# Attention forward and backward on one core: operands in quarter tiles, the normalisation's place, and where the constant matmuls stand

## The chip, the cores and the metric

The kernel runs on one core of a Trainium2 chip. The metric is device time in microseconds (us) of one execution. Five engines work side by side, each through its own instructions in order: TensorE (PE; PEld is its weight load), VectorE (DVE), ScalarE (ACT), GpSimd (POOL) and SyncE (SP), which in this kernel issues every DMA.

## The reference

The reference is the forward and backward pass of a gated mix of two branches over 2048 tokens of width 576. The changed part is branch A, an attention with 32 heads of width 18, and its gradients:

```python
qkv = (x @ wqkv).reshape(B, S, 3, H, Dh)          # S = 2048, H = 32, Dh = 18
scores = einsum("bhqd,bhkd->bhqk", q, k) * Dh ** -0.5
p = softmax(scores)
o = einsum("bhqk,bhkd->bhqd", p, v)
a = o.transpose(...).reshape(B, S, D) @ wo
...
return g * a + (1 - g) * b                        # g: a gate per token; b: an SSM convolution
```

The outputs are the result and the gradients of all inputs of both branches. Branch B, the projections and the weight gradients are other stages of the kernel and are not changed.

## The kernel before

The attention stage lies between 251 and about 2466 us of the profiled execution. Heads are padded to 32 columns, so a **group** g is four heads side by side on 128 partitions; there are 8 groups. Queries are cut into four blocks b of 512. A **unit** u = 4g + b is one group with one query block: 32 units, forward and backward. For a unit all 2048 keys are swept in 16 tiles i of 128.

The stage is one loop over a counter `G`. I call one turn of it a **half-step**; 32 half-steps (`NST`) are a unit. In one half-step the forward of unit u runs beside the backward of an earlier one, which is 39 half-steps behind (`OFF`, and `G2 = G - OFF`). PE, ACT, DVE and POOL run in the order in which the code records their instructions (`manual_schedule`). SP is not in that list: a scheduler orders the DMAs by its own estimate of when each is ready, and SP then works through that order one by one.

A half-step records, in this order:

- what was put off to it with `at(("pre", G), ...)`: gradient stores (`store_grad`: ACT copies `gb`, SP transposes it into `gT`, POOL copies it to `dtk`, SP stores that) and, once a unit, `f1` and `f2` (below);
- six score matmuls on PE, three kinds twice: P1 (key tile against the unit's queries, for the forward), P3 (query tile against 512 keys, for the backward) and P2 (value tile against `dOaT`). P1 and P3 share four PSUM buffers with the tag S, P2 has two with the tag dP;
- a **burst**: constant matmuls of `J_bf` with the identity (`fill`, `NFILL` of them; their result is written over or not used), and accumulations. The number `ph = G2 % 4` names four kinds of half-step, and four of them I call a cycle. In ph 0, the **value** half-step: accO (forward output, 4 matmuls), then accV (`dv_burst`, 8). In ph 1, the **query** half-step: accO, then accQ (`dq_burst`, 8). In ph 2, the **key** half-step: accK (`dk_half` twice, 16). In ph 3, the **free** half-step: only constants, into accF. accV, accQ, accK and accF share one PSUM bank (accB), and each burst starts with its `NFILL[ph]` constants;
- on ACT four exponentials of 128x512 (L611 for P1 into `PT`, L615 for P3 into `eb`), on DVE two products (L620, `ds` from P2's result and `PT`), whose transposes `dsT` SP issues (L626); then the evictions of the burst on DVE (`dvacc` L473, `dqa` L490, `dkacc` L514).

Once a unit, when accO is complete, `post_forward` gives three functions. `f0` copies accO to `oT` on ACT. `f1`, two half-steps later and ahead of the score matmuls, transposes `oT` back with four matmuls into `ps_o`, a PSUM buffer of the tag S, and then on DVE takes the reciprocal `rl` (L399), the normalised output `Ob` (L404) and the scaled output gradient `dOa` (L405). `f2`, one half-step later, multiplies the two into `prod` (L410), reduces it to `dl` (L412), writes that into `dOa` (L413) and issues two DMAs, the store `O_d` and the transpose `dOaT`, which the backward's P2 rows read from half-step 39 on.

`load_group(g)` brings a group's operands: `QaT`, `KaT` and `VaT` as they are and `Vtok`, `Ktok` and `Qtok` through a transposing DMA, each 128 x 2048 in one piece. All have two buffers but `Ktok` (read by accQ) and `Qtok` (read by accK), which have one. The load for the next group is recorded in a group's third unit.

Of the kernel before, what the change touches and what calls it, by code (L numbers as in the profile page):

```python
# [9 lines left out]
A = mybir.AluOpType  # L10
ACT = mybir.ActivationFunctionType
BF = mybir.dt.bfloat16
# [8 lines left out]
def build(tc, aps, dbg_aps=None, stages=("s1", "attn", "post", "s4", "final")):  # L21
# [39 lines left out]
    with ExitStack() as gctx:  # L61
# [281 lines left out]
        if "attn" in stages:  # L343
# [3 lines left out]
            DA = HP  # L347
            NFILL = (1, 1, 1, 4)
            with ExitStack() as ctx:
# [14 lines left out]

                def load_group(g):
                    T = {}
                    for nm, src, nb in (("QaT", QaT_d[g], 2), ("KaT", KaT_d[g], 2), ("VaT", VaT_d[g], 2)):
                        T[nm] = ga.tile([P, S], BF, tag=nm, bufs=nb, name=nm + "_g")
                        nc.sync.dma_start(T[nm], src)
                    for nm, src, nb in (("Vtok", VaT_d[g], 2), ("Ktok", KaT_d[g], 1), ("Qtok", QaT_d[g], 1)):  # L370
                        T[nm] = ga.tile([P, NT, 4, HP], BF, tag=nm, bufs=nb, name=nm + "_g")
                        nc.sync.dma_start_transpose(out=T[nm].rearrange("p t h w -> p t (h w)"), in_=src)
                    grp_t[g] = T

# [11 lines left out]
                def post_forward(g, b, acc):  # L386
                    U = UN[(g, b)]
                    st = {}

                    def f0():  # L390
                        st["oT"] = work.tile([P, KB], F32, tag="oT", bufs=1, name="oT")
                        nc.scalar.copy(st["oT"], acc)

                    def f1():
                        po = apsp.tile([P, TPQ, 4, HP], F32, tag="S", bufs=4, name="ps_o")
                        for qi in range(TPQ):
                            nc.tensor.transpose(po[:, qi, :, :].rearrange("p a b -> p (a b)"), st["oT"][:, qi * P:(qi + 1) * P], ident_f)
                        rl = work.tile([P, TPQ, 4], F32, tag="rl", bufs=1, name="rl")
                        nc.vector.reciprocal(rl, po[:, :, :, DH])  # L399
                        rlb = rl.unsqueeze(3).to_broadcast([P, TPQ, 4, DH])  # L400
                        Ob = work.tile([P, TPQ, 4, DH], BF, tag="Ob", bufs=1, name="Ob")
                        da = U["dOa"]
                        st["Ob"] = Ob
                        nc.vector.tensor_tensor(Ob, po[:, :, :, 0:DH], rlb, op=A.mult)  # L404
                        nc.vector.tensor_tensor(da[:, :, :, 0:DH], U["dO"], rlb, op=A.mult)  # L405

                    def f2():
                        da, Ob = U["dOa"], st["Ob"]
                        prod = work.tile([P, TPQ, 4, DH], F32, tag="prod", bufs=1, name="prod")
                        nc.vector.tensor_tensor(prod, da[:, :, :, 0:DH], Ob, op=A.mult)  # L410
                        dl = work.tile([P, TPQ, 4], F32, tag="dl", bufs=1, name="dl")
                        nc.vector.tensor_reduce(dl, prod, axis=AX.X, op=A.add)  # L412
                        nc.vector.tensor_scalar(da[:, :, :, DH], dl, -1.0, None, op0=A.mult)  # L413
                        nc.sync.dma_start(O_d[:, b * TPQ:(b + 1) * TPQ, 4 * g * DH:4 * (g + 1) * DH], Ob.rearrange("p t a b -> p t (a b)"))
                        U["dOaT"] = work.tile([P, TPQ, P], BF, tag="dOaT", name="dOaT")
                        nc.sync.dma_start_transpose(out=U["dOaT"], in_=U["dOa"].rearrange("p t a b -> p (t a b)"))
                    return f0, f1, f2
# [58 lines left out]
                def dq_burst(g, b, p):  # L476
                    U = UN[(g, b)]
                    acc = ACC.pop()
                    for n_ in range(2):
                        i = 2 * p + n_  # L480
                        for j in range(4):
                            mm(acc[HP * j:HP * (j + 1), :], lhsT=grp_t[g]["Ktok"][:, i, j, :], rhs=U["ds"][i][:, j, :],
                               start=(n_ == 0), stop=(n_ == 1), tile_position=(0, HP * j))
# [9 lines left out]
                def dk_half(g, b, p, h, st):  # L493
# [4 lines left out]
                    for qb in (2 * h, 2 * h + 1):  # L498
                        for j in range(4):
                            mm(acc[HP * j:HP * (j + 1), 0:2 * P].rearrange("p (a b) -> p a b", b=P), lhsT=grp_t[g]["Qtok"][:, b * TPQ + qb, j, :],  # L500
                               rhs=U["dsT", p][:, :, j * TPQ + qb, :], start=(qb == 0), stop=(qb == 3), tile_position=(0, HP * j))
# [14 lines left out]

                load_group(0)
                NTOT = NU * NST
                for G in range(NTOT + OFF + 16):
# [3 lines left out]
                    if G < NTOT:  # L523
# [5 lines left out]
                        if s == 4 and b == NQ - 2 and g + 1 < NG:  # L529
                            load_group(g + 1)  # L530
                        r1 = (g, b, s // 2, 2 * (s % 2))
# [8 lines left out]
                    for x in range(2):  # L540
                        if r1:
                            g, b, i, j0 = r1
                            T = grp_t[g]
                            rows.append(("P1", g, b, i, j0 + x, row("P1", g, b, T["KaT"][:, i * P:(i + 1) * P], T["QaT"][:, b * KB:(b + 1) * KB], j0 + x)))
                        if r2:
# [5 lines left out]
                            kq, ii = s2 // 8, (s2 % 8) // 2  # L551
                            qt = b * TPQ + ii
                            rows.append(("P3", g, b, (kq, ii), jo, row("P3", g, b, T["QaT"][:, qt * P:(qt + 1) * P], T["KaT"][:, kq * KB:(kq + 1) * KB], jo)))
                            i2 = s2 // 2
                            j2 = 2 * par_ + (1 - x)
                            rows.append(("P2", g, b, i2, j2, row("P2", g, b, T["VaT"][:, i2 * P:(i2 + 1) * P], U["dOaT"].rearrange("p t q -> p (t q)"), j2)))
                    evs = []
                    if G % 4 in (3, 0) and G >= 3:
                        i_ = (G - 3) // 4 * 2 + (1 if G % 4 == 0 else 0)
                        u_, i_ = divmod(i_, NT)  # L560
                        if u_ < NU:
# [3 lines left out]
                            for j in range(4):  # L565
                                mm(accO[(g, b)][HP * j:HP * (j + 1), :], lhsT=grp_t[g]["Vtok"][:, i_, j, :], rhs=UN[(g, b)]["PT"][i_][:, j, :],
                                   start=(i_ == 0), stop=(i_ == NT - 1), tile_position=(0, HP * j))
                            if i_ == NT - 1:
                                f0, f1, f2 = post_forward(g, b, accO.pop((g, b)))
                                evs.append(f0)  # L570
                                at(("pre", G + 2), f1)
                                at(("pre", G + 3), f2)
                    if ph in (0, 1, 2):
                        ACC.append(accB(("accV", "accQ", "accK")[ph]))
                        fill(ACC[0], NFILL[ph])
                    elif 0 <= G2 < NTOT:
                        fill(accB("accF"), NFILL[3])
                    if G2 % 4 == 0 and G2 >= 4:
# [27 lines left out]
                    for (kind, g, b, i, j, ps) in rows:  # L606
# [5 lines left out]
                        elif kind == "P3":  # L612
                            e = work.tile([P, KB], BF, tag="eb", bufs=10, name="eb")
                            U["eb"][(i[0], i[1], j)] = e
# [735 lines left out]
```

## Time and the profile before

| | |
|---|---|
| time, median of 9 runs | 3860.94 us (3854.22 to 3865.70) |
| the profiled execution | 3863.19 us, its span 3861.5 us |
| busy share of the span | PE 76%, DVE 75%, ACT 73%, POOL 2% |
| attention exponentials on ACT | 4096, 644 and 650 ns each by their rows |
| `ds` products on DVE | 2048, 686 ns each |
| constant matmuls | 256 each in accV, accQ and accK, 1040 in accF |

The span is the time from the first to the last instruction; 1.7 us of the execution lie around it. ACT and DVE overlap one instruction with the next, so a row's mean duration is longer than the distance between two of them. The distance between the ends of instructions that follow each other tells the pace.

### The profile page before, as it was taken

What the parts mean: (1) busy time and instruction counts of PE and PEld (TensorE: products, weight loads), DVE (VectorE), ACT (ScalarE), POOL (GpSimd) and SP (SyncE); (2) the same over time, 40 slices, a digit from 0 to 9 for tenths busy, and PEclk for the clock granted to TensorE, in tenths of its full rate; (3) what the DMA queues carried; (4) which work ended last, traced back from release to release, by engine and by line L of the source; (5) the groups of instructions that cost most, each with busy time, mean ns of one, the idle gap of its engine ahead of it and who ended that gap; (6) DMA issues with size and microseconds to landing.
All of it is one profiled execution on the core that took longest, in us unless ns stands there. A gap on an engine that the chain in (4) does not pass through costs nothing. (4 is left out here: it accounts for less than half of the span.)

```text
span 3861.5 us, 67450 instructions
## 1 busy us (share of the span) xinstructions
PE 2950.7 (76%) x25828; PEld 1164.3 (30%) x25828; DVE 2915.1 (75%) x5131; ACT 2830.8 (73%) x5253; POOL 62.8 (2%) x146
## 2 busy tenths in 40 slices
PE   7979999999989989989989999499244455444421
PEld 2312322323323323323223232146133333333320
DVE  4617877878878878878878888444388888888867
ACT  4549999999999999999989998310366666666610
POOL 0000000000000000000000000100000000000000
PEclk9959999999999999999999999789555555555555
DMA  8537788888887797887887887965455565655456
GB/s 198 166 99 126 139 159 144 143 159 142 145 162 136 142 165 138 143 163 136 145 159 135 147 145 135 242 155 135 84 98 106 106 108 111 113 97 103 84 147 198
DMA packets 1860151, 537.00 MB, mean 139 GB/s; under 512 B 1774991, under 2 KB 1838553, under 8 KB 1859826
## 3 DMA queue, kind: packets, MB, share of 16 engines
q1 hardware_dynamic: 1859826, 532.69, 71.8%
q8 instruction: 202, 3.31, 0.3%
q14 instruction: 123, 1.01, 0.1%
HBM read 99.74 MB, written 60.96 MB: 42 GB/s over the span
## 5 line engine op out<-in xcount | busy, mean ns | idle before, releaser
L620 DVE TENSOR_TENSOR ds<-ps_P,PT 128x512 bf16<-128x512 f32 x2048 | 1343.9, 686 | 181.9 <-PE ps_P L30 176.2
L611 ACT ACTIVATE PT<-ps_P 128x512 bf16<-128x512 f32 x2048 | 1308.3, 644 | 75.8 <-PE ps_P L30 68.5
L615 ACT ACTIVATE eb<-ps_P 128x512 bf16<-128x512 f32 x2048 | 1326.4, 650 | 22.6 <-PE ps_P L30 22.5
L30 PE MATMUL ps_P<-KaT_g,QaT_g 32*128 32x512 bf16 x2048 | 749.4, 384 | 55.8 <-ACT PT L611 4.4
L30 PE MATMUL ps_P<-dOaT,VaT_g 32*128 32x512 bf16 x2048 | 781.3, 390 | 5.9 <-DMA dOaT<-dOa 5.0
L30 PE MATMUL ps_P<-QaT_g,KaT_g 32*128 32x512 bf16 x2048 | 663.9, 392 | 18.9 <-DMA KaT_g<-KaT_d 5.8
L30 PEld LDWEIGHTS <-VaT_g 32*128 32x128 bf16 x2048 | 180.3, 91 | 368.6 <-issue 354.8
L30 PEld LDWEIGHTS <-J_bf 128*128 128x128 bf16 x1872 | 162.5, 98 | 397.9 <-issue 301.0
L30 PE MATMUL accF<-ident_bf,J_bf 128*128 128x512 bf16 x1040 | 277.6, 390 | 0.0
L30 PEld LDWEIGHTS <-KaT_g 32*128 32x128 bf16 x2048 | 122.1, 93 | 401.9 <-issue 388.3
L473 DVE TENSOR_TENSOR dvacc<-dvacc,accV 128x512 f32<-128x512 f32 x224 | 153.7, 686 | 95.2 <-PE accV L30 94.4
L30 PE MATMUL uvp<-RX,E1e 128*128 128x64 bf16 x1152 | 134.1, 290 | 107.6 <-DVE E1e L919 107.6
L30 PE MATMUL accO<-PT,Vtok_g 128*32 128x512 bf16 x2048 | 212.3, 399 | 0.0
L30 PE MATMUL tps<-RX,T0w 128*128 128x32 bf16 x576 | 38.4, 233 | 213.8 <-DVE yd L1054 190.4
L900 ACT ACTIVATE kk<-ph,magc 128x512 f32<-128x512 f32 x144 | 91.0, 685 | 147.6 <-DVE E1e L918 112.8
L30 PE MATMUL ph<-thr,lrow 3*128 3x512 bf16 x288 | 126.3, 567 | 87.9 <-ACT ab L893 60.5
L30 PEld LDWEIGHTS <-QaT_g 32*128 32x128 bf16 x2048 | 158.5, 91 | 112.0 <-issue 95.8
L30 PE MATMUL accK<-dsT,Qtok_g 128*32 128x256 bf16 x4096 | 164.5, 282 | 27.8 <-DMA Qtok_g<-QaT_d 25.1
L490 DVE TENSOR_TENSOR dqa<-dqa,accQ 128x512 f32<-128x512 f32 x224 | 153.9, 687 | 32.5 <-PE accQ L30 21.1
L30 PE MATMUL accQ<-ds,Ktok_g 128*32 128x512 bf16 x2048 | 160.0, 389 | 13.4 <-DMA Ktok_g<-KaT_d 13.4
L30 PEld LDWEIGHTS <-E1e 128*128 128x128 bf16 x1152 | 125.2, 123 | 128.3 <-DVE E1e L919 127.8
L30 PE MATMUL accV<-eb,dOa 128*32 128x512 bf16 x2048 | 157.8, 385 | 0.0
(271 smaller groups left out, 3767.6 us busy)
## 6 DMA issues: line engine op xcount, KB each, us to landing
T0w<-Kp_d SPq DMA_DIRECT2D x36, 512.0 KB
dsT<-ds SPq DMA_TRANSPOSE x512
dqkv_d<-dtk SPq DMA_DIRECT2D x96, 72.0 KB
dqkv_tok<-dqkv_d SPq DMA_DIRECT2D x1, 6912.0 KB
Md_d<-mst SPq DMA_DIRECT2D x144, 36.0 KB
ga_d<-ga_st SPq DMA_DIRECT2D x16, 288.0 KB
dxm_d<-dxm SPq DMA_DIRECT2D x16, 288.0 KB
skw<-Md_d SPq DMA_DIRECT2D x72, 64.0 KB
```

The costliest lines, as they stand in the source:

```text
L30: return nc.tensor.matmul(out, lhsT=lhsT, rhs=rhs, start=start, stop=stop, **kw)
L473: nc.vector.tensor_tensor(a_, a_, acc, op=A.add)
L490: nc.vector.tensor_tensor(U["dqa"], U["dqa"], acc, op=A.add)
L611: nc.scalar.activation(U["PT"][i][:, j, :], ps, ACT.Exp)
L615: nc.scalar.activation(e, ps, ACT.Exp)
L620: nc.vector.tensor_tensor(U["ds"][i][:, j, :], ps, U["PT"][i][:, j, :], op=A.mult)
L900: nc.scalar.activation(B_["kk"][h][:, 4 * q:4 * q + 4, :], ph, ACT.Identity, bias=magc, scale=1.0)
```

## The change

The change has these parts.

- `load_group` is replaced. `KaT` stays in one piece of 2048 columns with two buffers (`load_full`). The other five operands come in quarter pieces of 512 columns (`load_piece`), each a tile of its own, with 3 buffers for `QaT`, 5 for `VaT`, `Vtok` and `Ktok`, and 2 for `Qtok`. Each piece is recorded 14 to 20 half-steps ahead of the half-step for which it is listed. All readers take the piece.
- `f1` no longer runs ahead of the score matmuls. Its transposes go into the accF bank, behind the constants of the free half-step. `rl` and `Ob` stay on DVE, recorded after that half-step's `ds` products; `dOa` and `prod` move from DVE to POOL.
- `f2` no longer makes `prod`. It is recorded among the evictions of the next half-step, ahead of dvacc.
- `NFILL` goes from (1, 1, 1, 4) to (0, 1, 1, 5).
- `eb` gets 12 buffers in place of 10.

```diff
--- before.py
+++ after.py
@@ -345,7 +345,7 @@
             NQ = S // KB
             TPQ = KB // P
             DA = HP
-            NFILL = (1, 1, 1, 4)
+            NFILL = (0, 1, 1, 5)
             with ExitStack() as ctx:
                 ctx.enter_context(tc.manual_schedule(engines={mybir.EngineType.PE, mybir.EngineType.Activation, mybir.EngineType.DVE, mybir.EngineType.Pool}))
                 ga = ctx.enter_context(tc.tile_pool(name="ga", bufs=2))
@@ -362,15 +362,22 @@
                     dOa2.append(dOa_u)
                 grp_t = {}
 
-                def load_group(g):
-                    T = {}
-                    for nm, src, nb in (("QaT", QaT_d[g], 2), ("KaT", KaT_d[g], 2), ("VaT", VaT_d[g], 2)):
-                        T[nm] = ga.tile([P, S], BF, tag=nm, bufs=nb, name=nm + "_g")
-                        nc.sync.dma_start(T[nm], src)
-                    for nm, src, nb in (("Vtok", VaT_d[g], 2), ("Ktok", KaT_d[g], 1), ("Qtok", QaT_d[g], 1)):
-                        T[nm] = ga.tile([P, NT, 4, HP], BF, tag=nm, bufs=nb, name=nm + "_g")
-                        nc.sync.dma_start_transpose(out=T[nm].rearrange("p t h w -> p t (h w)"), in_=src)
-                    grp_t[g] = T
+                PB = {"QaT": 3, "VaT": 5, "Vtok": 5, "Ktok": 5, "Qtok": 2}
+
+                def load_full(g):
+                    t_ = ga.tile([P, S], BF, tag="KaT", bufs=2, name="KaT_g")
+                    nc.sync.dma_start(t_, KaT_d[g])
+                    grp_t.setdefault(g, {})["KaT"] = t_
+
+                def load_piece(nm, g, m):
+                    src = {"QaT": QaT_d, "VaT": VaT_d, "Vtok": VaT_d, "Ktok": KaT_d, "Qtok": QaT_d}[nm][g][:, m * KB:(m + 1) * KB]
+                    if nm in ("QaT", "VaT"):
+                        t_ = ga.tile([P, KB], BF, tag=nm, bufs=PB[nm], name=nm + "_g")
+                        nc.sync.dma_start(t_, src)
+                    else:
+                        t_ = ga.tile([P, TPQ, 4, HP], BF, tag=nm, bufs=PB[nm], name=nm + "_g")
+                        nc.sync.dma_start_transpose(out=t_.rearrange("p t h w -> p t (h w)"), in_=src)
+                    grp_t.setdefault(g, {})[nm, m] = t_
 
                 UN = {}
                 DKV = {}
@@ -391,23 +398,25 @@
                         st["oT"] = work.tile([P, KB], F32, tag="oT", bufs=1, name="oT")
                         nc.scalar.copy(st["oT"], acc)
 
-                    def f1():
-                        po = apsp.tile([P, TPQ, 4, HP], F32, tag="S", bufs=4, name="ps_o")
+                    def f1(po):
                         for qi in range(TPQ):
-                            nc.tensor.transpose(po[:, qi, :, :].rearrange("p a b -> p (a b)"), st["oT"][:, qi * P:(qi + 1) * P], ident_f)
-                        rl = work.tile([P, TPQ, 4], F32, tag="rl", bufs=1, name="rl")
-                        nc.vector.reciprocal(rl, po[:, :, :, DH])
-                        rlb = rl.unsqueeze(3).to_broadcast([P, TPQ, 4, DH])
-                        Ob = work.tile([P, TPQ, 4, DH], BF, tag="Ob", bufs=1, name="Ob")
-                        da = U["dOa"]
-                        st["Ob"] = Ob
-                        nc.vector.tensor_tensor(Ob, po[:, :, :, 0:DH], rlb, op=A.mult)
-                        nc.vector.tensor_tensor(da[:, :, :, 0:DH], U["dO"], rlb, op=A.mult)
+                            nc.tensor.transpose(po[:, qi * P:(qi + 1) * P], st["oT"][:, qi * P:(qi + 1) * P], ident_f)
+                        po = po.rearrange("p (t a b) -> p t a b", a=4, b=HP)
+
+                        def ev():
+                            rl = work.tile([P, TPQ, 4], F32, tag="rl", bufs=1, name="rl")
+                            nc.vector.reciprocal(rl, po[:, :, :, DH])
+                            rlb = rl.unsqueeze(3).to_broadcast([P, TPQ, 4, DH])
+                            Ob = st["Ob"] = work.tile([P, TPQ, 4, DH], BF, tag="Ob", bufs=1, name="Ob")
+                            nc.vector.tensor_tensor(Ob, po[:, :, :, 0:DH], rlb, op=A.mult)
+                            da = U["dOa"]
+                            nc.gpsimd.tensor_tensor(da[:, :, :, 0:DH], U["dO"], rlb, op=A.mult)
+                            prod = st["prod"] = work.tile([P, TPQ, 4, DH], F32, tag="prod", bufs=1, name="prod")
+                            nc.gpsimd.tensor_tensor(prod, da[:, :, :, 0:DH], Ob, op=A.mult)
+                        return ev
 
                     def f2():
-                        da, Ob = U["dOa"], st["Ob"]
-                        prod = work.tile([P, TPQ, 4, DH], F32, tag="prod", bufs=1, name="prod")
-                        nc.vector.tensor_tensor(prod, da[:, :, :, 0:DH], Ob, op=A.mult)
+                        da, Ob, prod = U["dOa"], st["Ob"], st["prod"]
                         dl = work.tile([P, TPQ, 4], F32, tag="dl", bufs=1, name="dl")
                         nc.vector.tensor_reduce(dl, prod, axis=AX.X, op=A.add)
                         nc.vector.tensor_scalar(da[:, :, :, DH], dl, -1.0, None, op0=A.mult)
@@ -479,7 +488,7 @@
                     for n_ in range(2):
                         i = 2 * p + n_
                         for j in range(4):
-                            mm(acc[HP * j:HP * (j + 1), :], lhsT=grp_t[g]["Ktok"][:, i, j, :], rhs=U["ds"][i][:, j, :],
+                            mm(acc[HP * j:HP * (j + 1), :], lhsT=grp_t[g]["Ktok", i // TPQ][:, i % TPQ, j, :], rhs=U["ds"][i][:, j, :],
                                start=(n_ == 0), stop=(n_ == 1), tile_position=(0, HP * j))
 
                     def ev():
@@ -497,7 +506,7 @@
                     acc = st["acc"]
                     for qb in (2 * h, 2 * h + 1):
                         for j in range(4):
-                            mm(acc[HP * j:HP * (j + 1), 0:2 * P].rearrange("p (a b) -> p a b", b=P), lhsT=grp_t[g]["Qtok"][:, b * TPQ + qb, j, :],
+                            mm(acc[HP * j:HP * (j + 1), 0:2 * P].rearrange("p (a b) -> p a b", b=P), lhsT=grp_t[g]["Qtok", b][:, qb, j, :],
                                rhs=U["dsT", p][:, :, j * TPQ + qb, :], start=(qb == 0), stop=(qb == 3), tile_position=(0, HP * j))
                     if h == 0:
                         return None
@@ -514,7 +523,18 @@
                             nc.vector.tensor_tensor(a_[:, sl], a_[:, sl], acc[:, 0:2 * P], op=A.add)
                     return ev
 
-                load_group(0)
+                load_full(0)
+                lds = []
+                for g in range(NG):
+                    for m in range(4):
+                        g0 = 4 * g * NST
+                        lds += [(g0 + NST * m - 14, "QaT", g, m), (g0 + 8 * m - 20, "Vtok", g, m), (g0 + OFF + 8 * m - 20, "VaT", g, m),
+                                (g0 + OFF + 8 * m - 18, "Ktok", g, m), (g0 + OFF + NST * m - 14, "Qtok", g, m)]
+                for g0, nm, g, m in sorted(lds):
+                    if g0 < 0:
+                        load_piece(nm, g, m)
+                    else:
+                        at(("pre", g0), lambda nm=nm, g=g, m=m: load_piece(nm, g, m))
                 NTOT = NU * NST
                 for G in range(NTOT + OFF + 16):
                     for f in todo.pop(("pre", G), []):
@@ -527,7 +547,7 @@
                             new_unit(g, b)
                             accO[(g, b)] = None
                         if s == 4 and b == NQ - 2 and g + 1 < NG:
-                            load_group(g + 1)
+                            load_full(g + 1)
                         r1 = (g, b, s // 2, 2 * (s % 2))
                     G2 = G - OFF
                     if 0 <= G2 < NTOT:
@@ -541,7 +561,7 @@
                         if r1:
                             g, b, i, j0 = r1
                             T = grp_t[g]
-                            rows.append(("P1", g, b, i, j0 + x, row("P1", g, b, T["KaT"][:, i * P:(i + 1) * P], T["QaT"][:, b * KB:(b + 1) * KB], j0 + x)))
+                            rows.append(("P1", g, b, i, j0 + x, row("P1", g, b, T["KaT"][:, i * P:(i + 1) * P], T["QaT", b], j0 + x)))
                         if r2:
                             g, b, s2 = r2
                             T = grp_t[g]
@@ -549,11 +569,10 @@
...
-                            qt = b * TPQ + ii
-                            rows.append(("P3", g, b, (kq, ii), jo, row("P3", g, b, T["QaT"][:, qt * P:(qt + 1) * P], T["KaT"][:, kq * KB:(kq + 1) * KB], jo)))
+                            rows.append(("P3", g, b, (kq, ii), jo, row("P3", g, b, T["QaT", b][:, ii * P:(ii + 1) * P], T["KaT"][:, kq * KB:(kq + 1) * KB], jo)))
                             i2 = s2 // 2
                             j2 = 2 * par_ + (1 - x)
-                            rows.append(("P2", g, b, i2, j2, row("P2", g, b, T["VaT"][:, i2 * P:(i2 + 1) * P], U["dOaT"].rearrange("p t q -> p (t q)"), j2)))
+                            rows.append(("P2", g, b, i2, j2, row("P2", g, b, T["VaT", i2 // TPQ][:, (i2 % TPQ) * P:(i2 % TPQ + 1) * P], U["dOaT"].rearrange("p t q -> p (t q)"), j2)))
                     evs = []
                     if G % 4 in (3, 0) and G >= 3:
                         i_ = (G - 3) // 4 * 2 + (1 if G % 4 == 0 else 0)
@@ -563,18 +582,23 @@
                             if i_ == 0:
                                 accO[(g, b)] = apsp.tile([P, KB], F32, tag="accO", name="accO")
                             for j in range(4):
-                                mm(accO[(g, b)][HP * j:HP * (j + 1), :], lhsT=grp_t[g]["Vtok"][:, i_, j, :], rhs=UN[(g, b)]["PT"][i_][:, j, :],
+                                mm(accO[(g, b)][HP * j:HP * (j + 1), :], lhsT=grp_t[g]["Vtok", i_ // TPQ][:, i_ % TPQ, j, :], rhs=UN[(g, b)]["PT"][i_][:, j, :],
                                    start=(i_ == 0), stop=(i_ == NT - 1), tile_position=(0, HP * j))
                             if i_ == NT - 1:
                                 f0, f1, f2 = post_forward(g, b, accO.pop((g, b)))
                                 evs.append(f0)
-                                at(("pre", G + 2), f1)
-                                at(("pre", G + 3), f2)
+                                at(("f1", G + 2), f1)
+                                at(("f2", G + 3), f2)
                     if ph in (0, 1, 2):
                         ACC.append(accB(("accV", "accQ", "accK")[ph]))
                         fill(ACC[0], NFILL[ph])
-                    elif 0 <= G2 < NTOT:
-                        fill(accB("accF"), NFILL[3])
+                    elif 0 <= G2 < NTOT or ("f1", G) in todo:
+                        acc_f = accB("accF")
+                        fill(acc_f, NFILL[3])
+                        for f in todo.pop(("f1", G), []):
+                            evs.append(f(acc_f))
+                    for f in todo.pop(("f2", G), []):
+                        evs.append(f)
                     if G2 % 4 == 0 and G2 >= 4:
                         p_ = (G2 - 4) // 4
                         if p_ < NTOT // 4:
@@ -610,7 +634,7 @@
                                 U["PT"][i] = ptp.tile([P, 4, KB], BF, tag="PT", name="PT")
                             nc.scalar.activation(U["PT"][i][:, j, :], ps, ACT.Exp)
                         elif kind == "P3":
-                            e = work.tile([P, KB], BF, tag="eb", bufs=10, name="eb")
+                            e = work.tile([P, KB], BF, tag="eb", bufs=12, name="eb")
                             U["eb"][(i[0], i[1], j)] = e
                             nc.scalar.activation(e, ps, ACT.Exp)
                         else:
```

## The prediction

> **What bounds it now.** A "faster" or "slower" below means a move of more than 0.2% (7.7 us), about what a measurement of this kernel can tell from no change. The page's slices put PE and ACT at nine tenths from about 250 to 2456 us, the attention stage that the change touches. There I read the timeline of one cycle of four half-steps (start, duration, engine, line, operation):
>
> ```profile
> 1002.77 1.04 PE L30 MATMUL accF<-ident_bf,J_bf 128*128 128x512 bf16 x4
> ...
> 1003.69 0.67 ACT L615 ACTIVATE eb<-ps_P 128x512 bf16<-128x512 f32 x1
> ...
> 1003.74 0.38 PE L30 MATMUL ps_P<-QaT_g,KaT_g 32*128 32x512 bf16 x1
> ...
> 1004.16 0.69 ACT L611 ACTIVATE PT<-ps_P 128x512 bf16<-128x512 f32 x1
> ...
> 1004.41 0.37 PE L30 MATMUL ps_P<-KaT_g,QaT_g 32*128 32x512 bf16 x1
> ...
> 1004.73 0.40 PE L30 MATMUL accO<-PT,Vtok_g 128*32 128x512 bf16 x4
> ...
> 1005.06 0.39 PE L30 MATMUL accV<-ident_bf,J_bf 128*128 128x512 bf16 x1
> ...
> 1005.38 0.61 PE L30 MATMUL accV<-eb,dOa 128*32 128x512 bf16 x8
> ...
> 1005.61 0.71 ACT L615 ACTIVATE eb<-ps_P 128x512 bf16<-128x512 f32 x1
> ...
> 1005.93 0.38 PE L30 MATMUL ps_P<-QaT_g,KaT_g 32*128 32x512 bf16 x1
> ...
> 1006.35 0.60 ACT L611 ACTIVATE PT<-ps_P 128x512 bf16<-128x512 f32 x1
> ```
>
> Read ACT by its ends (start plus duration): 1004.36, then 1004.85. An exponential ends every 0.49 us, so a half-step of four takes 1.96. The one exception in the cycle: 1006.32 is followed by 1006.95, 0.14 late. So ACT bounds, and 0.14 us in each cycle of 7.98 is a loop with PE. The loop: the last score row of a half-step starts 0.05 after the exponential that frees its S buffer (1004.36, 1004.41); the burst starts 0.32 later (1004.73); the next row comes after the burst's length B (1005.93, B = 1.20); its exponential ends 1.02 later (1006.95). From a half-step's first exponential to the first one two half-steps on, that is 3 x 0.49 + 0.05 + 0.32 + B + 1.02 = 2.86 + B, against 8 x 0.49 = 3.92 for ACT alone. A burst above 1.06 us stalls ACT by the rest. Value and query bursts both have B = 1.20 and overlap in one half-step, so they share one 0.14. The free half-step has B = 0.97 (1002.77 to 1003.74), 0.09 under the limit.
>
> Next, unit boundaries and the waits:
>
> ```profile
> PE accK L30 <- DMA Qtok_g<-QaT_d: 25.1, 6, 5.7
> ...
> PEld L30 <- DMA Ktok_g<-KaT_d: 15.5, 7, 3.2
> ```
>
> Unit lengths, from the first L611 of one unit to that of the next: 65.2 us where nothing else happens (units 6, 7, 10, 11 and so on), 67.0 in the first unit of a group (four extra gradient copies on ACT), but 76.4, 75.4, 76.6, 75.5, 76.4, 79.2 and 70.7 in units 5, 9, 13, 17, 21, 25 and 29, which also have four copies. Ktok and Qtok have one buffer each, so the new group's load waits for the old group's last use.
>
> **Part 1, quarter tiles loaded ahead.** The seven units sum to 530.2; at 67.0 each they would be 469.0. Excess: 61 us, which holds the two waits, the late dOaT (SP is behind), and the clock that is lower after them. With five quarter buffers for Ktok and Vtok and two for Qtok, the loads are issued 14 to 20 half-steps (over 27 us) ahead, so I take all of it: -61. Cost: 168 load issues instead of 48, all on SP. A quarter transpose is as large as gT's, 1.53 us on SP; the full ones took 4.28 (Ktok), 2.99 (Qtok), 1.96 (Vtok). Per group 12 x 1.53 against 9.2, and some seven more copies of about 0.4: +12 us of SP in some 270, where SP is busy 0.55 to 0.8 of a unit. What is queued behind are the dsT transposes; between a pair's second dsT issue and its use lie 7 to 13 us in the units shown, so I cost this at nothing; if that cover went, 1.5 us per piece would show. At the start KaT now goes first, the query quarter after a transpose: about 0.
>
> **Part 2, constant matmuls 1,1,1,4 to 0,1,1,5.** In the value burst the constant matmul takes 1005.06 to 1005.38, 0.32: B falls to 0.88, no stall. But the query burst keeps 1.20, so its 0.14 stays; it is no longer shared. In the free half-step constants start 0.216 apart ((1.04 - 0.39) / 3): B = 0.97 + 0.216 = 1.19, a new stall of 0.13. These two bursts do not share a half-step. So +0.125 a cycle, 1.0 us a unit. In the 14 units with extra copies each 0.49 copy on ACT covers a stall, about half: 17 x 1.0 + 14 x 0.5 = +24 us. Bounds: 0 if something overlaps the fifth one, 31 if nothing is covered.
>
> **Part 3, normalisation in the free half-step, two products on Pool.**
>
> ```profile
> 1234.45 0.66 PE L397 MATMUL ps_o<-ident_f,oT 128*128 128x128 f32 x4
> ...
> 1235.14 0.26 DVE L399 RECIPROCAL rl<-ps_o 128x16 f32<-128x16 f32 x1
> ...
> 1235.81 0.45 DVE L405 TENSOR_TENSOR dOa<-dO_b,rl 128x288 bf16<-128x288 bf16 x1
> ...
> 1237.38 0.45 DVE L410 TENSOR_TENSOR prod<-dOa,Ob 128x288 f32<-128x288 bf16 x1
> ...
> 1237.91 0.60 ACT L611 ACTIVATE PT<-ps_P 128x512 bf16<-128x512 f32 x1 [0.29 <-PE ps_P L30]
> ```
>
> Removed: ps_o holds an S buffer and comes ahead of the rows; ACT ends 0.89 after the exponential before it there (1237.62 to 1238.51), a stall of 0.40 a unit. Added: the four transposes (0.59 from 1234.45 to the next row) sit behind five constants, B = 1.19 + 0.59 = 1.78, stall 2.86 + 1.78 - 3.92 = 0.72, of which 0.13 is in part 2: +0.19 net. Then f2's reduction on DVE waits for prod from Pool, and the four ds and dvacc behind it wait too, with the accB bank and PE's query burst after that. Pool has no two-operand product here. Its rows: dtk's copy of the same 288 elements at 427 ns; low end 0.43 each (DVE's two-operand and copy rows cost alike), high end 1.28 (three passes of 0.43). I take two passes, 0.85, since it reads two operands.
>
> ```profile
> L426 POOL COPY dtk<-gT 128x288 bf16<-128x288 bf16 x96 | 41.0, 427 | 2180.6 <-DMA gT<-gb 2180.6
> ```
>
> From the reciprocal: 0.26 + 2 x 0.85 + 0.2 of hops = 2.16; DVE itself is busy 0.30 + 0.40 + two ds at 0.62 = 1.94. A wait of 0.2, half of it swallowed: +0.1. Together 0.29 x 32 = +9. At 0.43 there is no wait (+6); at 1.28 it is 0.86 more per unit (+37).
>
> [...]
>
> Pool is in order. In the second unit of each group (seven times) the gradient copy dtk of value block 2 is recorded just ahead of f1's products, and it waits for gb and the gT transfer: in before's trace 2.8 to 5.4 us from gb's end to dtk's start, mean 4.0. Products end at 4.0 + 0.43 + 1.7 + 0.15 = 6.3 after gb; DVE arrives at f2 at about 3.6 (2.1 in before, plus 1.3 for the later place, plus 0.2). Wait 2.7, less an idle stretch of DVE of 0.65 a cycle: 2.0 x 7 = +14. PE stands for it. After the waits of 2.41 and 2.74 us on Ktok and Qtok in unit 9 the granted clock was 0.86 and 0.76:
>
> ```profile
> 848.00:856.00 8.00, 7.65 (x62) 2.13 (x62) 6.39 (x11) 7.29 (x15) 0.85 (x2) 0.86 0.90 172
> 856.00:870.00 14.00, 11.16 (x88) 2.66 (x85) 7.75 (x13) 9.53 (x20) 0.43 (x1) 0.76 0.82 136
> ```
>
> The half-steps after them were 0.3 to 1.5 us long; 0.7 x 7 = +5. [...] f2's DMAs: O_d and dOaT follow about 1.3 us later; the first product row came 6.8 after f2's end, and dOaT needs under 5, so nothing. More eb buffers: nothing waits for them.
>
> **Sum.** -61 + 24 + 9 + 14 + 5 = -9. The profiled execution took 3863.2 (span 3861.5) and stands 2.3 above the median: 3854 on its terms, 3852 on the median's.
>
> **Rivals.** (a) Slower: Pool's products. Each 0.1 us more per product costs 2 x 32 x 0.1 = 6.4 us in DVE's wait; from 0.99 each the gain is gone, from 1.11 it is slower, at 1.28 it is 3861 - 9 + 27 = 3879. For it: no such row exists; against: the copy's 427 ns. (b) Quarter loads do not free the group change: SP in order waits for a freed buffer (KaT, query quarter) or for dqkv_d and delays dsT; half of the 61 comes back, 3882. Against: 7 to 13 us of cover. (c) The fifth constant is free: 0.09 of cover in the loop for it, its 0.216 against; 3852 - 24 = 3828. (d) The change does nothing in sum, since its terms differ in sign: 3861.
>
> **How the numbers follow.** Forecast 0.40 (its own range 3840 to 3862), (a) 0.25, (b) 0.10, (c) 0.15, (d) 0.10. Faster than 3853.2: 0.24 of the forecast, all of (c), 0.06 of the rest, 0.45. Within 0.2%: 0.16 of the forecast and 0.09 of (a), (b) and (d), 0.25. Slower: 0.30. The range, down to near (c) and up to (a) and (b): 3831 to 3882.
>
> **What would show it.** Right: units 5, 9 and so on without waits for Ktok and Qtok; clean units of about 66.5; ACT ends 0.63 apart after both query and free half-steps; in second units one wait of DVE for prod of 2 to 3 us. Wrong: Pool rows of TENSOR_TENSOR over 1 us, DVE waiting for prod in all 32 units, waits for dsT or dOaT, a granted clock under 1.00 in clean units, or a cycle still of 7.98.

## The result and the profile after

The changed kernel takes 3877.1 us (median of 9 runs, 3868.11 to 3879.51), against 3861.5 for the kernel before (median of 29 runs): ratio 1.0038, 95% interval 1.0030 to 1.0047. It is slower, by 15 us. The profiled execution has a span of 3875.4 us against 3861.5. The forecast was 9 us faster; the time lies inside its range, on the other side of no change.

First the waits, in the window of attention from 300 to 2460 us (engine, what it waits for, us in total, times, longest):

```profile
ACT PT L635 <- PE ps_P L30: 62.4, 38, 7.7
...
DVE dl L421 <- POOL prod L415: 40.6, 7, 6.7
```

The waits of PE for Ktok and Qtok are gone. A new one stands in their place: seven times, once in the second unit of each group after the first, DVE waits for Pool's `prod`, 5.8 us on average, and ACT then runs dry for up to 7.7 us.

The unit lengths say where the time sits. Each is the distance from the first L635 (L611 before) of a unit to that of the next (for unit 31, the last, to its last L635 but one), and the sums are in us. First and second units are those of a group, from the second group on; clean units are the fifteen others from unit 2 to unit 30. The rows below the first two are the runs of the next section:

| kernel | seven second units (5, 9, ... 29) | seven first units (4, 8, ... 28) | fifteen clean units | unit 1 | unit 31 |
|---|---|---|---|---|---|
| before | 530.1 | 468.9 | 978.3 | 60.2 | 63.0 |
| after | 523.4 | 472.5 | 990.9 | 63.5 | 64.1 |
| loads alone | 508.2 | 468.9 | 978.3 | 60.3 | 63.0 |
| normalisation alone | 536.1 | 469.1 | 978.4 | 62.2 | 63.0 |
| after, constants put back | 522.9 | 469.1 | 978.4 | 61.9 | 63.0 |
| loads alone, SP's queue in recorded order | 471.7 | 468.9 | 978.4 | 61.4 | 63.0 |
| after, SP's queue in recorded order | 490.4 | 472.4 | 990.9 | 63.3 | 64.1 |
| loads, recorded order, constants (0, 0, 1, 4) | 467.8 | 467.4 | 967.0 | 59.2 | 63.0 |

From before to after: -6.7 + 3.6 + 12.6 + 3.3 + 1.1 = +13.9, which is the whole difference of the spans. So the constants show up as forecast (a clean unit goes from 65.22 to 66.06), and the second units, which were to give 61 less some 19 (and some 3 for the constants), gave 6.7.

Now the pace of a cycle, from the timeline of a clean unit after:

```profile
1005.51 0.67 ACT L639 ACTIVATE eb<-ps_P 128x512 bf16<-128x512 f32 x1
1006.21 0.60 ACT L635 ACTIVATE PT<-ps_P 128x512 bf16<-128x512 f32 x1
...
1009.57 0.67 ACT L639 ACTIVATE eb<-ps_P 128x512 bf16<-128x512 f32 x1
1010.26 0.60 ACT L635 ACTIVATE PT<-ps_P 128x512 bf16<-128x512 f32 x1
```

Ends at 1006.18 and 1006.81, then 1010.24 and 1010.86: 0.63 and 0.62 apart, twice in a cycle, two half-steps from each other. Before there was one such step. These are the two stalls that the prediction's sum for a pair of half-steps, 2.86 + B against 3.92, had asked for.

Pool's products, from the groups by line (busy us, mean ns of one, idle before):

```profile
L415 POOL TENSOR_TENSOR prod<-dOa,Ob 128x288 f32<-128x288 bf16 x32 | 22.1, 690 | 2.5
L413 POOL TENSOR_TENSOR dOa<-dO_b,rl 128x288 bf16<-128x288 bf16 x32 | 21.6, 674 | 1047.3 <-DVE rl L408 1047.3
```

They are quicker than the 0.85 us of the forecast, and in clean units DVE does not wait for them at all: its seven waits for `prod` are those of the second units. For these products of 288 elements, 674 and 690 ns on Pool stand against 449 ns each on DVE before (L405, L410), 1.5 times.

Last, SP's queue (SPq: an issue by SP) and what hangs on it, from the timeline of unit 5 after:

```profile
548.67 1.50 SPq L433 DMA_TRANSPOSE gT<-gb  x1
...
551.85 0.86 ACT L431 ACTIVATE gb<-dvacc 128x512 bf16<-128x512 f32 x1
551.99 0.36 SPq L436 DMA_DIRECT2D dqkv_d<-dtk  x1
552.45 3.08 SPq L650 DMA_TRANSPOSE dsT<-ds  x1
...
555.62 1.22 SPq L379 DMA_TRANSPOSE Ktok_g<-KaT_d  x1
...
556.93 1.22 SPq L433 DMA_TRANSPOSE gT<-gb  x1
...
559.51 0.43 POOL L435 COPY dtk<-gT 128x288 bf16<-128x288 bf16 x1 [7.54 <-DMA gT<-gb]
...
560.65 0.69 POOL L415 TENSOR_TENSOR prod<-dOa,Ob 128x288 f32<-128x288 bf16 x1
...
561.37 0.45 DVE L421 TENSOR_REDUCE dl<-prod 128x16 f32<-128x288 f32 x1 [5.12 <-POOL prod L415]
...
562.68 0.59 PE L30 MATMUL accQ<-ident_bf,J_bf 128*128 128x512 bf16 x1 [5.22 <-DVE dvacc L482]
...
564.81 0.60 ACT L635 ACTIVATE PT<-ps_P 128x512 bf16<-128x512 f32 x1 [6.16 <-PE ps_P L30]
```

Read it from the bottom. ACT waits 6.16 us for a score row, because PE's query burst stood 5.22 for `dvacc`, and DVE, which evicts it, 5.12 for `prod`; `prod` is behind `dtk` in Pool's order; `dtk` waits for the transfer `gT`; and SP issues `gT` only at 556.93, though ACT had finished `gb` at 552.71. In these 4.2 us SP was at work on a `dsT` transpose and on a quarter of Ktok, one of the new loads. Just before, from 550.17 to 551.99, it had issued nothing: the store `dqkv_d` stood at the head of the queue and waited for an earlier `dtk`, and the `dsT` came behind it. The same stretch before:

```profile
546.99 0.86 ACT L422 ACTIVATE gb<-dvacc 128x512 bf16<-128x512 f32 x1
548.14 1.29 SPq L424 DMA_TRANSPOSE gT<-gb  x1
...
552.53 0.43 POOL L426 COPY dtk<-gT 128x288 bf16<-128x288 bf16 x1 [7.37 <-DMA gT<-gb]
```

There SP took `gT` 0.3 us after `gb` ended (547.85 to 548.14). Over the seven group changes, for this one gradient block, means in us from the end of `gb`:

| kernel | SP issues gT | dtk starts on Pool |
|---|---|---|
| before | 0.71 | 3.98 |
| normalisation alone | 0.57 | 3.75 |
| loads alone | 4.58 | 7.39 |
| after | 4.60 | 7.48 |
| loads alone, SP's queue in recorded order | 0.10 | 2.77 |
| after, SP's queue in recorded order | 0.12 | 2.78 |

The 4.60 us after are, in the mean, 1.96 of `dsT`, 1.65 of a Ktok quarter, 0.29 of a store and 0.70 without an issue; the 0.71 before are 0.62 of `dsT` and the step to the next issue. SP was not later with everything: each second unit has four more gradient blocks, whose `gT` came, in the mean of each, 4.6 to 9.1 us after `gb` before and 2.4 to 4.8 after. The lateness moved to the block on which Pool's products hang.

### The profile page after: what moved, and what is told of

Read it like the earlier page. It is cut to its first block, busy times and chain, and to the rows that moved or that the text cites. A ratio compares the mean times of both kernels' runs of the same rounds, so it can differ in the third digit from the quotient of the medians.

```text
span 3875.4 us, 67760 instructions
## 1 busy us (share of the span) xinstructions
PE 2931.0 (76%) x25837; PEld 1164.2 (30%) x25837; DVE 2885.0 (74%) x5067; ACT 2840.2 (73%) x5253; POOL 106.1 (3%) x210
## 5 line engine op out<-in xcount | busy, mean ns | idle before, releaser
L635 ACT ACTIVATE PT<-ps_P 128x512 bf16<-128x512 f32 x2048 | 1306.3, 643 | 79.8 <-PE ps_P L30 68.6
L30 PE MATMUL ps_P<-QaT_g,KaT_g 32*128 32x512 bf16 x2048 | 688.7, 390 | 36.8 <-DMA QaT_g<-QaT_d 5.8
L30 PE MATMUL accF<-ident_bf,J_bf 128*128 128x512 bf16 x1305 | 330.7, 384 | 0.0
L30 PEld LDWEIGHTS <-QaT_g 32*128 32x128 bf16 x2048 | 144.9, 91 | 168.8 <-issue 161.1
```

What stands on the lines that cost most here:

```text
L30: return nc.tensor.matmul(out, lhsT=lhsT, rhs=rhs, start=start, stop=stop, **kw)
L635: nc.scalar.activation(U["PT"][i][:, j, :], ps, ACT.Exp)
```

## The experiments

The ratios are to the kernel before, run beside each on the same chip (median 3866.3 in the first four, 3869.6 in the others), with 95% intervals.

### The gradient store one half-step later

The first theory was Pool's order: `dtk` ahead of the products. Recorded one half-step later, the store of a value block comes behind them.

```diff
-    at(("pre", G + 3), lambda g=g, kq=q_ // 2: store_grad(DKV.pop(("v", g, kq)), ...))
+    at(("pre", G + 4), lambda g=g, kq=q_ // 2: store_grad(DKV.pop(("v", g, kq)), ...))
```

> The changed kernel with one number different: the gradient store of a value block is recorded one half-step later, so that its Pool copy dtk stands behind the normalisation's two products in Pool's order and not ahead of them. Theory (Pool's order: the products wait for a gradient copy that waits for its transfer): the wait of DVE for prod, 40.6 us in seven places, goes; units 5, 9 and so on fall from 74.8 us in the mean to about 67.5 like the first units of a group, the total by 7 x 7.3 = 51 us, to about 3826. Rival (the stall comes from SP, which reaches dOaT and dsT late, or from slow Pool products): those units stay at 73 to 75 and the total within 8 us of 3877.

Measured: 3886.09, ratio 1.0048 (1.0034 to 1.0061), no better than after. DVE's wait for `prod` fell from 40.6 to 9.2 us in all, but the second units stayed at 73.7 to 77.2, with a wait that after does not have:

```profile
PE ps_P L30 <- DMA dOaT<-dOa: 22.2, 7, 4.6
```

Now the transpose `dOaT`, which also stands in SP's queue, comes late and P2 waits. So Pool's order passes the lateness on, and taking the products out from behind `dtk` brought no time. The edit moves the whole store, ACT's copy and `gT` with it, so it is no test of Pool's order alone.

### The products back on DVE

```diff
-    nc.gpsimd.tensor_tensor(da[:, :, :, 0:DH], U["dO"], rlb, op=A.mult)
+    nc.vector.tensor_tensor(da[:, :, :, 0:DH], U["dO"], rlb, op=A.mult)
...
-    nc.gpsimd.tensor_tensor(prod, da[:, :, :, 0:DH], Ob, op=A.mult)
+    nc.vector.tensor_tensor(prod, da[:, :, :, 0:DH], Ob, op=A.mult)
```

> The changed kernel with dOa and prod back on DVE; f1's place, the constants and the loads stay. Theory (Pool's order): DVE's wait goes in the seven units, -51 us; DVE takes 0.37 + 0.48 us more in every unit, of which I expect 0.2 to 0.3 to show in 32 units, +8: about 3834, clean units 66.1 to 66.4. Rival (DVE's own load at this place is what stalls, and Pool helped): clean units over 66.6 and the total above 3845. Rival (SP late): total within 8 us of 3877.

Measured: 3899.15, ratio 1.0083 (1.0065 to 1.0100): worse than after, a miss by 65 us. Second units 71.0 to 73.4, again with a `dOaT` wait (19.7 us in all), and clean units 66.9 to 67.8 instead of 66.06: with the normalisation at this place the two products cost 0.9 to 1.7 us a unit on DVE. So at this place Pool is the better engine for them; over the kernel before, the normalisation's move as a whole gains nothing (see the normalisation alone, below). The granted clock tells 0.9 from 1.7, here in two clean units:

```profile
626.14:693.07 66.93, 62.92 (x573) 19.77 (x572) 55.38 (x96) 65.20 (x132) 0.43 (x1) 1.00 0.79 138
693.07:760.79 67.72, 64.04 (x573) 19.90 (x572) 55.61 (x96) 65.19 (x132) 0.43 (x1) 0.97 0.81 142
```

The third column from the right is TensorE's granted clock. Clean units that keep 1.00 take 66.92, 0.86 over 66.06 and about what the two products last (0.9); those with 0.97 take 67.5 to 67.8.

### The constants put back

```diff
-            NFILL = (0, 1, 1, 5)
+            NFILL = (1, 1, 1, 4)
```

> The changed kernel with the constant matmuls at 1, 1, 1, 4 as in the kernel before. Theory (the pair rule, 2.86 us + B): ACT's ends are late once a cycle by 0.14 and not twice; clean units fall from 66.06 to about 65.1, units with four more copies by 0.5; total -21 us, to about 3856. The waits of the seven units stay. Rival (constants in the free half-step are covered): clean units stay at 66.0 and the total at 3877.

Measured: 3856.24, ratio 0.9973 (0.9963 to 0.9983). Clean units are 65.22 again. The move of the constants costs 19 us by the unit lengths (12.5 + 3.4 + 0.5 + 1.6 + 1.1), and (1.0038 - 0.9973) x 3861 = 25 by the ratios.

### The loads alone

The kernel before with the quarter loads, and nothing else of the change.

> The kernel before with only the loads in quarter tiles; normalisation, constants and eb as before. Theory: the waits for Ktok and Qtok go and nothing takes their place, units 5, 9 and so on fall from 75.7 us in the mean to about 67.0; total -61 us, 3800. Rival (quarter pieces put on SP ahead of gT and dsT delay those, which was the changed kernel's loss): units 5, 9 and so on stay above 70, and the total above 3825.

Measured: 3842.07, ratio 0.9934 (0.9917 to 0.9950). The rival held: second units fall from 75.7 to 72.6 on average, not to 67. What is late next, from the waits and the timeline of unit 5:

```profile
PE ps_P L30 <- DMA dOaT<-dOa: 25.0, 7, 4.2
```

```profile
549.42 1.98 SPq L379 DMA_TRANSPOSE Ktok_g<-KaT_d  x1
551.50 1.22 SPq L431 DMA_TRANSPOSE gT<-gb  x1
...
554.60 0.36 SPq L434 DMA_DIRECT2D dqkv_d<-dtk  x1
555.05 1.40 SPq L643 DMA_TRANSPOSE dsT<-ds  x1
556.54 1.97 SPq L423 DMA_TRANSPOSE dOaT<-dOa  x1
```

DVE begins the reduction of f2 at 548.36, and SP reaches `dOaT` at 556.54. Ahead of it are the Ktok quarter, `gT`, and the store `dqkv_d`, which waits for `dtk` at the head of the queue while SP issues nothing else (0.7 us, 553.89 to 554.60). Without Pool in the chain the same lateness of SP therefore costs through `dOaT`.

### The normalisation alone

The kernel before with f1 and f2 as in the change, loads in whole groups, constants (1, 1, 1, 4).

> The kernel before with one part of the change alone: the normalisation in the group before the burst with its two products on Pool, loads in whole groups as before, constants (1, 1, 1, 4). Theory: Pool holds DVE up in the second units only because the quarter loads make SP late with the gradient transposes; with whole-group loads SP issues them within 1.5 us, so DVE waits for the product at most 3 us in each of the seven second units, clean units stay at 65.2 to 65.4 us, the time is 3850 to 3875 (the Ktok and Qtok waits are still there). Rival (Pool's order is the cost by itself, whoever is late): DVE waits over 5 us for the product in each second unit, time 3885 to 3905.

Measured: 3871.54, ratio 1.0006 (0.9995 to 1.0017): no difference. Clean units 65.22 to 65.23. The wait for `prod`:

```profile
DVE dl L414 <- POOL prod L408: 16.1, 7, 3.0
```

2.3 us each, where after has 5.8. So the wait that Pool's order makes by itself is near the 2.7 of the forecast, though the second units grew by 6.0 us in all and not by 19. That the rest of the wait in after is SP's is tested below, with SP's queue in recorded order on the whole change. Clean units sum to 978.4 against 978.3 before, so they gain nothing by it.

### SP's queue in recorded order, on the loads alone

```diff
-    engines={... mybir.EngineType.Pool}
+    engines={... mybir.EngineType.Pool, mybir.EngineType.SP}
...
-    PB = {"QaT": 3, "VaT": 5, "Vtok": 5, "Ktok": 5, "Qtok": 2}
+    PB = {"QaT": 3, "VaT": 8, "Vtok": 8, "Ktok": 8, "Qtok": 2}
...
-    nc.sync.dma_start(dqkv_d[...], dtk...)
+    at(("pre", CUR[0] + 2), lambda: nc.sync.dma_start(dqkv_d[...], dtk...))     # CUR[0] is G
...
-    (g0 + 8 * m - 20, "Vtok", g, m), (g0 + OFF + 8 * m - 20, "VaT", g, m), (g0 + OFF + 8 * m - 18, "Ktok", g, m)
+    (g0 + 8 * m - 52, "Vtok", g, m), (g0 + 8 * m - 50, "VaT", g, m), (g0 + 8 * m - 24, "Ktok", g, m)     # for g > 0
```

> The kernel before with the quarter loads (as in the run of the loads alone, ratio 0.993), and SP's queue in a recorded order: a group's VaT, Vtok and Ktok quarters get 8 buffers and are issued in the third and fourth unit of the group before, and the store of a finished gradient block is issued two half-steps after its transpose instead of right behind it, so SP does not stand waiting for Pool's copy. Theory (SP's in-order queue is what kept 5 us in every second unit): second units 67 to 68.5 us where they were 72.6, the dOaT wait under 1 us each, time 3842 - 7 x 4.6 = 3810 (3800 to 3822). Rival (the dOaT chain is bounded by something else: DVE's products, the transfer itself, or the clock after the burst): second units stay over 71, time 3835 to 3850.

Measured: 3811.68, ratio 0.9852 (0.9836 to 0.9868), as the theory had it. All seven second units are 67.4 us long. SP takes `gT` when `gb` is done (551.50 to 551.53):

```profile
550.64 0.86 ACT L429 ACTIVATE gb<-dvacc 128x512 bf16<-128x512 f32 x1
551.53 1.19 SPq L431 DMA_TRANSPOSE gT<-gb  x1
```

SP's time in its issues, summed over its DMA rows in the trace, is 78% of the second units before, 77% after, 81% with the loads alone and 76% here. So SP was no fuller after than before: what had changed there is what stands ahead of what. From the loads alone to this run more than the order changes. The edit has two halves, the order with its later store and the loads moved out to the third and fourth unit, and the second takes work away: SP has 51.5 us of it in such a unit here, 58.6 with the loads alone. The halves were not run apart, and which one carries the gain is open.

### The same on the whole change

> The changed kernel with the same order of SP's queue as the run before it. Theory: the waits of the changed kernel's second units came from SP, so DVE's wait for Pool's product falls from 5.8 to at most 2 us in each second unit, second units 68 to 70 us (74.8 in the changed kernel), clean units stay at 66.06, time 3877 - 7 x 5.8 = 3836 (3825 to 3848). Rival (the gradient copy ahead of the products in Pool's order costs this by itself): the wait stays over 4 us each, time over 3860.

Measured: 3848.38, ratio 0.9952 (0.9937 to 0.9967), that is 33 us under after by the ratios and just past the upper end of what the theory expected. Second units 68.4 to 71.7, and of DVE's wait is left:

```profile
DVE dl L421 <- POOL prod L415: 8.9, 8, 1.7
```

The wait falls from 5.8 to 1.1 us each, so SP's lateness made most of it in this kernel too. The run is 37 us above the one before it: 12.5 of that lie in clean units (the constants) and 18.7 in second units. Most of the latter goes with the granted clock, which is 1.00 in two of the seven; here is one of them, and the one with the lowest:

```profile
1096.53:1164.97 68.44, 63.91 (x573) 20.06 (x572) 54.76 (x93) 67.05 (x136) 3.88 (x8) 1.00 0.84 149
1364.57:1436.30 71.73, 67.84 (x573) 20.31 (x572) 54.81 (x93) 67.37 (x136) 3.88 (x8) 0.90 0.82 144
```

The two take 68.4, 1.0 more than the 67.4 of the run before it, which would be 7 us in seven units; the other 11.5 lie in the five units with a clock of 0.90 to 0.98 (70.0 to 71.7 us). Whether the constants or Pool's order set off these drops is open.

### Fewer constants

The loads with SP's queue in recorded order, and this edit:

```diff
-            NFILL = (1, 1, 1, 4)
+            NFILL = (0, 0, 1, 4)
```

> The run with SP's queue in recorded order on top of the loads alone, with constants (0, 0, 1, 4) instead of (1, 1, 1, 4): one matmul less in the value and in the query half-step, 0.22 us each at full clock. Theory (a burst that is longer than 1.06 us stalls ACT, and the value and the query burst are the ones above it): 65.2 goes to about 64.2 us per clean unit, so some 30 us less than the run with (1, 1, 1, 4): 3780. Rival (the constants hold TensorE's clock): the granted clock in attention falls below what the same run with (1, 1, 1, 4) shows, and the time is the same or longer than there, 3810 to 3900.

Measured: 3793.55, ratio 0.9809 (0.9794 to 0.9824): the quickest version here, 2.3% under the changed kernel by the ratios. Both sides were partly right. Clean units are 64.12 where nothing happens, but of 29 units (2 to 30) 13 show a granted clock of 0.95 to 0.97, where the same run with (1, 1, 1, 4) shows 1.00 in every one, and a clean one of these is up to 1.8 us longer. Of the 30 us expected 17 came, by the ratios.

## Why the prediction was wrong

**The step that failed** is the cost of Part 1 on SP: "so I cost this at nothing". Its cover, 7 to 13 us, was read for `dsT` alone. Two other transposes stand in the same queue and have far less: `gT`, which Pool's order ties to DVE, and `dOaT`, dismissed with "dOaT needs under 5, so nothing". The Ktok quarters are issued as their old buffers come free (some 10 half-steps ahead of their place in the code), three of a group's four within 14 half-steps of the start of the second unit, just where the finished gradients are stored, and SP's `gT` went from 0.71 to 4.60 us after `gb`. For `dOaT` the prediction's own figures, 6.8 us and under 5, left some 2 us of cover; with the loads alone SP issued it 7.8 us after f2's last row in the second units, against 4.2 before, and PE waited 25 us for it in all. The runs show the price from both ends: with the loads alone 530.1 - 508.2 = 22 us of the 61 came, with SP's queue in recorded order and the loads moved 530.1 - 471.7 = 58. The gain was there, as sized; some 36 us of it were lost in SP's queue. This is rival (b), which had 0.10, in its kind: SP in order, and the store `dqkv_d` at its head. But it named `dsT` as what comes late, and half of the 61 as the loss; so its 3882 near the measured 3877 is in part luck, as is the 3879 of rival (a), whose slow products did not come.

**The sum added terms that depend on each other.** The Pool-queue term (+14, with +5 for the clock after the waits) was worked out from the 4.0 us between `gb` and `dtk` in the trace of before. With before's loads the wait came out right, 2.7 forecast and 2.3 measured, but not its price: the second units grew by 6.0 in all, with the waits for Ktok and Qtok still beside it. But Part 1 makes those 4.0 into 7.5, and the wait 5.8. Second units without these waits are 67.4 us, and about 0.5 more with the moved constants (an estimate: the first units grew by that), so 523.4 - 7 x 67.9 = 48 us of waits and their after-effects stand where 19 were forecast. A change to one queue has to be carried into every delay that the other terms read from it.

**The clock after the waits** is in those 48 us. The windows of unit 5 after, with the granted clock in the third column from the right:

```profile
553.00:561.00 8.00, 4.29 (x36) 1.68 (x35) 2.30 (x5) 5.64 (x12) 1.41 (x3) 0.91 0.87 148
561.00:566.00 5.00, 3.32 (x24) 0.64 (x27) 4.13 (x8) 1.19 (x3) 0.34 (x1) 0.50 0.87 140
```

Half the clock, for 5 us after the wait. That is no sharper a drop than the one from which the forecast took its 0.7 us per group: its 0.76 is the mean of 14 us, and in the kernel before the clock stood at half for nearly half of them:

```profile
860.48:867.31 6.83, 6.46 (x45) 1.51 (x45) 3.00 (x5) 4.12 (x8) 0.43 (x1) 0.50 0.71 97
```

Nor is the clock lower after than before: over the seven second units it is 0.91 to 0.96 before and 0.93 to 0.95 after, and 1.00 in each of them in the loads with SP's queue in recorded order. The 61 us of Part 1 held the price of such drops by the prediction's own words, and after has them back. How much of the 48 us is theirs, no run here shows, so the +5 can't be told from the rest.

**Part 2, the constants (+24), was right**: 19 to 25 us, by the mechanism given. Two steps of 0.63 and 0.62, stalls of 0.14 and 0.13, stand where one of 0.14 was shared, a clean unit grows by 0.84 where 1.0 was forecast, and a first unit by 0.5, half a cover as said.

**Part 3 in clean units (+9) was too high**: 0.29 was forecast for a unit, and the fifteen clean units sum to 978.4 with it and 978.3 without. Pool's products take 0.67 to 0.69 us, inside the bounds of 0.43 and 1.28, and DVE does not stand for them there. Rival (a), slow products, is out: the two passes taken, 0.85 us, were too high. The +0.19 per unit for the transposes behind the constants did not show; unit 1 alone grew, by 2.0.

**The balance.** Forecast -9, measured about +15. Second units: -38.5 forecast (-61 + 14 + 5 + 7 x 0.5), -6.7 measured, so 32 us worse. All the rest was 7 to 9 us better than forecast (29.5 us were forecast for it, and 21 by the unit lengths or 22 by the medians were measured). That the time lies in the stated range is therefore luck in part: the two errors have opposite signs, and the range had been drawn to take in its rivals.

## What to carry to other kernels

A queue that works in order, as SP's did here (a store at its head held it for 1.8 us, 550.17 to 551.99), is a resource with a head: when transfers are added to it, ask of every transfer behind them when its reader needs it, and take the one with the least cover, not the largest. Splitting loads so that they start early brought what it promised here (58 of the 61 us, against 22) only when the queue had a recorded order, nothing at its head that waited for another engine, and the loads outside the stretch in which it is already fed; which of these is needed was not shown. Terms that read a delay from the old trace are not independent of a part of the change that alters that delay.

## What the runs showed of the hardware

TensorE's granted clock fell to 0.50 without a wait of PE over 0.4 us. With constants (0, 0, 1, 4), in a clean unit, windows of 4 us (PE busy in the first group of numbers after the length; the granted clock third from the right):

```profile
1212.00:1216.00 4.00, 3.82 (x44) 1.22 (x32) 3.15 (x6) 4.00 (x10) 0.00 (x0) 1.00 0.89 172
1216.00:1220.00 4.00, 3.64 (x29) 0.92 (x25) 3.46 (x6) 4.00 (x10) 0.00 (x0) 0.93 1.19 161
1220.00:1224.00 4.00, 4.00 (x29) 1.11 (x27) 2.46 (x5) 3.22 (x7) 0.43 (x1) 0.50 0.80 150
```

PE was busy for 3.64 of the 4 us in which the drop began, no wait of PE or of its weight loads between 1200 and 1222 us was longer than 0.4 us, and the clock still went to 0.50. In two kernels no clean unit shows a drop; PE is busy there for 97% of such a unit (63.29 of 65.2 us, constants 1, 1, 1, 4) and 95% (62.79 of 66.06, the changed kernel). In two others some clean units show one; those without have 94.5% (60.60 of 64.1, constants 0, 0, 1, 4) and 94% (62.92 of 66.93, the products back on DVE). But the share alone does not tell the units with a drop: with (0, 0, 1, 4) the second unit from 539.80 to 606.10 kept 1.00 at 93% (61.79 of 66.3). What sets off the drop, these runs do not show. With SP's queue in recorded order all units from 2 to 30 kept 1.00 at (1, 1, 1, 4), and 13 of 29 had 0.95 to 0.97 at (0, 0, 1, 4); the run with those drops is still 17 us quicker by the ratios, so the two constants that it leaves out cost more than the drops.
